# Nyström attention and MLP on one core: another order table, a bf16 landmark softmax, and the first half-sums of k taken the other way round

## The chip, the cores and the metric

The kernel runs on one core of one Trainium2 chip. The core has five engines with a queue each: TensorE (PE, matrix multiply), VectorE (DVE), ScalarE (ACT), GpSimd (POOL) and SyncE (SP, which here only issues transfers). Each engine takes its instructions in the order in which the program lists them; engines wait for one another through semaphores. Transfers between the chip's memory and the core are issued by SP, POOL or ACT and are carried by 16 DMA engines. The metric is the device time of one execution in microseconds (us), the median over runs.

## What is computed

The reference chains a Nyström approximation of attention and a squared-ReLU MLP:

```python
q_lm = q.reshape(B, H, m, S // m, D).mean(axis=3)      # B = H = 8, S = 576, D = 64, m = 32
k_lm = k.reshape(B, H, m, S // m, D).mean(axis=3)
A, Bm, C = sm(q, k_lm), sm(q_lm, k_lm), sm(q_lm, k)    # softmax of a @ b.T / sqrt(D)
Z = Bm.T / (norm_1(Bm) * norm_inf(Bm) + 1e-06)
for _ in range(6):
    Z = 2 * Z - Z @ Bm @ Z
x = (A @ Z @ C @ v)                                    # then (B*S, H*D) = (4608, 512)
out = relu(x @ w_in) ** 2 @ w_out                      # w_in 512 x 2048, w_out 2048 x 512
```

The inputs and the output are float32; the kernel works in bfloat16 with float32 sums and is allowed the difference.

## The kernel before

The 8 batches go through one after the other, and batch b + 1's attention is mixed into batch b's MLP. `attention(b)` does the following, with "turn" counting the repetitions of a tag inside one batch:

- The landmarks. Batches 0 and 1 sum q and k over their segments on PE (`l_sum`, 9 matmuls for each half of the heads, line 544), move the sums out of PSUM (`l_ev`), fold them (`l_fold`, line 554) and duplicate them (`l_dup`). PE also transposes q and k (`tr`, `trk`, line 579, 3 turns of 6 each) and ACT or DVE moves these out (`trev`). Later batches use DVE transposes and adds instead (`hx`, `lmt`, `add9` to `add0h`).
- The 32 x 32 landmark softmax Bm: matmul `bmq`, maximum `nmb`, exponential `Eb` on ACT, reciprocal `rr` of the row sums, product `BB` (line 631), transpose `BTf` (line 633), cast `BTc` (line 634), column sums `cs`, their maximum `mx`, `cc`, reciprocal `rc` (line 651). From these come the first iterate's halves `st0z` (line 667) and `st0p` (line 669, from the matmul `p0`).
- Six Newton steps: matmul `nv` on PE (line 689 in batch 0, 694 later), update `upd` on DVE (line 704), the last one `upd5`.
- Beside them the scores of C (`c_mm`, `nmc`, `c_exp`, transposes `c_tr`, copies `c_ev`), the product with v (`cv`, `cv_ev`) and with Z (`wt`), and the scores of A (`a_mm`, `a_t`, `a_max`, `a_sub`, `a_exp`, `a_sum`, `a_rec`, `a_mul`, transpose `a_xp` into AT).
- Four `g_mm` matmuls multiply the attention's right-hand factor with the four quarters of w_in; eight `g_ev` copies move the result to the tile G.

`mlp_in(b)` then makes 16 blocks: `in_mm` (4 matmuls AT with G, line 948), `relu` (ACT line 965 or DVE line 967) and `square` (ACT line 973, DVE or POOL line 975). `mlp_out(b)` multiplies the blocks with w_out (`o_mm`, line 1020), copies the result (`o_ev`, lines 304 and 306) and stores it.

The order of all this isn't left to a scheduler. `ORDER` is a list of numbers, one for each operation: number // 64 is the operation, number // 8 % 8 its engine (0 PE, 1 ACT, 2 DVE, 3 POOL, 4 SP) and number % 8 its first PSUM bank. A negative number is a run of "fills": matmuls of a zero tile that write to a bank nobody reads (line 455); -480 is 60 of them. `PACE` gives an operation one more wait, on the last instruction of another operation. `Plan.emit` goes through the list and writes out each operation in turn:

```python
for code in order:
    if code < 0:
        self.fill((-code) % 8, (-code) // 8)
        continue
    op, e = self.ops[code // 64], ENGINES[code // 8 % 8]
    ...
        if op.idx in pace:
            wait(mine[0], last[pace[op.idx]])
```

Loads: the first half of batch 0's k comes through SP in two pieces into a float32 stage and is cast by ACT (`first_k`, `cast_k`). Every other load of k and q (two halves, 288 KB each as written), of v (four quarters, 144 KB each), of w_in (four quarters, 512 KB each, line 406) and of w_out (four quarters, line 414) is issued by POOL, in the order of the table, and a POOL load waits for the eighth POOL load before it, whose semaphore it takes over.

Of the kernel before, what the change touches and what calls it, by code (L numbers as in the profile page):

```python
# [8 lines left out]
P = 128  # L9
# [11 lines left out]
M = 32  # L21
# [155 lines left out]
]  # L177

PACE = {
# [908 lines left out]
```

## Time and profile before

| | us |
|---|---|
| median of 3 runs | 260.05 (259.89 to 260.05) |
| the profiled execution | 259.81 |
| its span, first to last instruction | 257.7 |
| PE busy / DVE / ACT / POOL | 245.8 / 206.0 / 199.5 / 143.6 |

The span is what the profile shows; 2.1 us of the execution lie around it. Busy time is the time in which at least one instruction of the engine ran; a fill counts as busy. The views used are the page (busy times, slices, the chain that ended last, groups), the table of stretches (busy time of each engine between two moments), the timeline (instructions in order of time, with the idle time before and what ended it in brackets), and the waits of one engine.

### The profile page before, as it was taken

How to read it: one execution, taken by the hardware profiler on the slowest of the kernel's cores; microseconds unless marked ns; L12 is line 12 of the kernel's file. 1: busy time of each engine (PE TensorE's matmuls, PEld its weight loads, DVE VectorE, ACT ScalarE, POOL GpSimd, SP SyncE). 2: the span in 40 equal slices, each digit the busy share in tenths (PEclk: the TensorE clock that was granted, in tenths of full speed). 3: DMA queues.
4: the chain of work that ended last, by engine and by line, in shares of the span. 5: the costliest groups of instructions: out<-in, count | busy, mean ns of one | idle time of the engine just before them, and what ended most of it. 6: DMA issues, size and time to landing. Idle time of an engine off the chain costs nothing.

```text
span 257.7 us, 7805 instructions
## 1 busy us (share of the span) xinstructions
PE 245.8 (95%) x3018; PEld 147.1 (57%) x3057; DVE 206.0 (80%) x496; ACT 199.5 (77%) x412; POOL 143.6 (56%) x216
## 2 busy tenths in 40 slices
PE   8879899999999999999999999999999999999994
PEld 8766655645654665545545565556645555466552
DVE  0489799999998998999989998888989878944221
ACT  3365799998998899888997798788977778667410
POOL 8446875775694457865587657926172554213300
PEclk9999999999999999999999999999999999999999
DMA  6999999459902980197505972493311432023023
GB/s 158 208 200 194 191 210 205 83 82 169 226 6 47 190 177 20 17 204 140 133 17 84 207 147 55 66 190 96 67 23 23 106 79 48 0 53 91 21 82 124
DMA packets 20468, 28.59 MB, mean 111 GB/s; under 512 B 3280, under 2 KB 11728, under 8 KB 20432
## 3 DMA queue, kind: packets, MB, share of 16 engines
q0 software_dynamic: 13296, 18.06, 43.9%
q1 hardware_dynamic: 6992, 9.90, 13.7%
q8 instruction: 24, 0.39, 0.6%
q10 hardware_dynamic: 144, 0.13, 0.2%
q14 instruction: 12, 0.10, 0.1%
HBM read 36.70 MB, written 9.44 MB: 179 GB/s over the span
## 4 chain that ended last, share of the span: by engine, by line
PE 82%; DMA 6%; DVE 5%; issue 2%; ACT 2%; POOL 1%; DVEq 0%; POOLq 0%; ACTq 0%
PE ps L1020 46%; PE ps L948 23%; DMA kraw<-in_k_dram 3%; PE ps L926 3%; DMA qraw<-in_q_dram 2%; PE ps L725 2%; PE ps L803 2%; PE ps L694 1%; PE ps L781 1%; PE ps L579 1%; PE ps L544 1%; PE ps L455 1%; DVE mxA L888 1%; ACT r L965 1%; POOL w_in_bf L406 1%
## 5 line engine op out<-in xcount | busy, mean ns | idle before, releaser
L1020 PE MATMUL ps<-w_out_bf,gs 128*128 128x512 bf16 (+1 forms) x553 | 138.7, 373 | 2.9 <-issue 1.3
L965 ACT ACTIVATE r<-ps 128x576 bf16<-128x576 f32 x108 | 68.3, 652 | 16.2 <-PE ps L948 13.6
L1020 PEld LDWEIGHTS <-gs 128*128 128x128 bf16 x592 | 53.3, 98 | 47.1 <-issue 7.3
L948 PE MATMUL ps<-AT,G 128*128 128x288 bf16 x512 | 77.5, 286 | 0.5 <-ACT Eb L626 0.2
L948 PEld LDWEIGHTS <-G 128*128 128x128 bf16 x512 | 49.2, 98 | 24.7 <-issue 1.1
L973 ACT ACTIVATE gs<-r 128x576 bf16<-128x576 bf16 x84 | 55.9, 685 | 1.0 <-DVE r L967 0.3
L975 POOL TENSOR_TENSOR gs<-r 128x576 bf16<-128x576 bf16 x24 | 27.6, 1157 | 24.4 <-ACT o L304 9.8
L379 POOL DMA_DIRECT2D vraw<-in_v_dram x32 | 18.2, 571 | 16.8 <-PE ps L725 3.8
L304 ACT CAST G<-ps 128x512 bf16<-128x512 f32 x44 | 23.5, 597 | 3.6 <-PE ps L926 3.5
L304 ACT COPY o<-ps 128x512 f32<-128x512 f32 (+1 forms) x27 | 15.1, 571 | 12.0 <-PE ps L1020 12.0
L967 DVE TENSOR_SCALAR r<-ps 128x576 bf16<-128x576 f32 x20 | 15.0, 751 | 9.8 <-PE ps L948 9.3
L901 POOL TENSOR_TENSOR EA<-EA,rA 128x576 bf16<-128x576 bf16 x15 | 17.4, 1161 | 3.0 <-DVE rA L899 1.1
L533 DVE STREAM_TRANSPOSE qT<-qraw 128x1152 bf16<-128x1152 bf16 x12 | 16.3, 1359 | 0.0
L533 DVE STREAM_TRANSPOSE kT<-kraw 128x1152 bf16<-128x1152 bf16 x12 | 16.2, 1347 | 0.0
L306 DVE CAST G<-ps 128x512 bf16<-128x512 f32 x20 | 13.2, 684 | 2.8 <-PE ps L926 2.8
L306 DVE COPY o<-ps 128x512 f32<-128x512 f32 x10 | 6.8, 685 | 10.6 <-PE ps L1020 10.6
L455 PE MATMUL ps<-zero 128*128 128x128 bf16 x149 | 13.1, 245 | 2.0 <-DVE zero L464 1.1
L890 POOL TENSOR_TENSOR SA<-SA,mxA 128x576 f32<-128x576 f32 x11 | 12.8, 1162 | 3.7 <-DVE Pd L638 2.2
L746 ACT ACTIVATE EC<-ps,nmc 128x288 bf16<-128x288 f32 x24 | 11.7, 499 | 3.8 <-DVE nmc L739 1.5
L704 DVE SCALAR_TENSOR_TENSOR st<-st,ps 128x128 bf16<-128x128 bf16 x40 | 11.0, 276 | 4.1 <-PE ps L694 3.4
L455 PEld LDWEIGHTS <-zero 128*128 128x128 bf16 x149 | 10.8, 112 | 3.6 <-issue 2.2
L884 DVE STREAM_TRANSPOSE SA<-ps 128x576 f32<-128x576 f32 x16 | 11.9, 764 | 1.1 <-PE ps L725 0.6
(146 smaller groups left out, 360.5 us busy)
## 6 DMA issues: line engine op xcount, KB each, us to landing
out_dram<-o SPq DMA_DIRECT2D x126, 64.0 KB, 2.5
qraw<-in_q_dram POOLq DMA_DIRECT2D x16, 288.0 KB, 6.6
vraw<-in_v_dram POOLq DMA_DIRECT2D x32, 144.0 KB, 6.3
kraw<-in_k_dram POOLq DMA_DIRECT2D x15, 288.0 KB, 6.2
w_in_bf<-in_moe_w_in_dram POOLq DMA_DIRECT2D x4, 512.0 KB, 8.1
w_out_bf<-in_moe_w_out_dram POOLq DMA_DIRECT2D x4, 512.0 KB, 9.7
out_dram<-o SPq DMA_DIRECT2D x3, 256.0 KB, 2.3
gs<-in_k_dram SPq DMA_DIRECT2D x2, 288.0 KB, 4.2
```

The source lines that it names most:

```text
L304: nc.scalar.copy(dst, src)
L306: ENG[e].tensor_copy(dst, src)
L379: nc.gpsimd.dma_start(vraws[z][p0:p0 + 32, :, :, :].rearrange("p g t d -> p g (t d)"), src[b].rearrange(order, i=2, t=SEG)[i, :, :, c * NJ ...
L455: mm(ps[:, bank, 0:P], lhsT=zero[:], rhs=zero[:], start=True, stop=True)
L533: add("hx", "DVE", lambda e, nm=nm, raw=raw, i=i: nc.vector.transpose(heads(nm)[:, i, :, :, :].rearrange("p t h r -> p (t h r)"), raw[:, i ...
L901: keep("a_mul", add("a_mul", "POOL DVE", lambda e, part=part, spread=spread: ENG[e].tensor_tensor(part(EA), part(EA), spread(part(rA)), AL ...
L948: mm(t[:, j, 0:HALF], lhsT=G[:, i, f * P:(f + 1) * P], rhs=AT[:, i, j * HALF:(j + 1) * HALF], start=(i == 0), stop=(i == 1))
L965: nc.scalar.activation(r.rearrange("p (j t) -> p j t", j=2), src, AF.Relu)
L967: nc.vector.tensor_scalar(out=r.rearrange("p (j t) -> p j t", j=2), in0=src, scalar1=0.0, scalar2=None, op0=ALU.max)
L973: nc.scalar.activation(dst, r[:], AF.Square)
L975: ENG[e].tensor_tensor(dst, r[:], r[:], ALU.mult)
L1020: mm(one(ok)[:, 0:hi - lo], lhsT=gs[:, f, x0:x0 + P], rhs=w_out_bf[:, f, lo:hi], start=(f == f0), stop=(f == f1 - 1))
```

## The change

Four things change in the code; line numbers after it are one or two lower.

```diff
-    BB = sb.tile([P, 2, M], F32, name="BB")
+    BB = sb.tile([P, 2, M], BF16, name="BB")
...
-    BTf = sb.tile([P, 2, M], F32, name="BTf")
...
-                for i in range(2):
+                for n, i in enumerate((1, 0) if nm == "k" and b == 0 else (0, 1)):
...
-                        writes=[lp, (nm, "lp", i)], acq=None if i else ("n", lp))
+                        writes=[lp, (nm, "lp", i)], acq=None if n else ("n", lp))
...
-            BTf.rearrange("p a m -> p (a m)"), BB.rearrange("p a m -> p (a m)")), reads=["BB"], writes=["BTf"])
-        add("BTc", "DVE ACT", lambda e: copy(e, BTc[:], BTf[:]), reads=["BTf"], writes=["BTc"])
+            BTc.rearrange("p a m -> p (a m)"), BB.rearrange("p a m -> p (a m)")), reads=["BB"], writes=["BTc"])
...
-        add("cs", "DVE", lambda e: nc.vector.reduce_sum(sm["cs"][:], BTf[:], axis=AX.X),
-            reads=["BTf"], writes=["cs"])
+        add("cs", "DVE", lambda e: nc.vector.reduce_sum(sm["cs"][:], BTc[:], axis=AX.X),
+            reads=["BTc"], writes=["cs"])
...
+        add("rq", "DVE", lambda e: nc.vector.tensor_tensor(sm["rq"][:], sm["rr"][:], sm["rc"][:], ALU.mult),
+            reads=["rr", "rc"], writes=["rq"])
...
-        add("st0z", "DVE", lambda e: nc.vector.tensor_tensor(s0[:, :, 1, :], BB[:], bcast(sm["rc"]), ALU.mult),
-            reads=["BB", "rc"], writes=[("st", 0, 1)])
+        add("st0z", "DVE", lambda e: nc.vector.tensor_tensor(s0[:, :, 1, :], Eb[:], bcast(sm["rq"]), ALU.mult),
+            reads=[("Eb", 0), ("Eb", 1), "rq"], writes=[("st", 0, 1)])
```

The fourth is the whole of `ORDER` and `PACE`. The old table has 196 pace waits, the new one 192. Decoded, the beginning of POOL's list reads (kX.h is half h of batch X's k, vX.n a quarter of v, wi and wo the quarters of w_in and w_out, `<-` a pace wait):

```
before: k0.1  q0.0  q0.1  ident  v0.3  q1.0  q1.1  v0.2  v0.0  wi.0  const4  k1.0  v0.1  wi.1<-cc
        a_sub.0  wi.2<-upd.0  k1.1<-a_t.1  a_sub.1  wi.3<-a_sum.0  a_mul.0  wo.0  wo.1  v1.2  k2.1  square ...
after:  q0.0  k0.1  ident  q0.1  const4  q1.0  q1.1  k1.1  k1.0  v0.1  v0.0  v0.2  v0.3<-BB  wi.0<-st0z
        a_sub.0  wi.1<-nmc.0  wi.2<-a_t.1  a_sub.1  wi.3<-upd.3  a_mul.0  a_mul.1  wo.0<-a_xp.0  wo.1  v1.0 ...
```

and the beginning of PE's, up to the first `in_mm`, batch and turn behind the tag, fills in brackets:

```
before: [60] tr.0.0 trk.0.2 l_sum.0.2 l_sum.0.0 l_sum.0.1 tr.0.2 l_sum.0.3 l_fold.0.0 tr.0.1 trk.0.0 trk.0.1
        bmq.0 a_mm.0.0 a_mm.0.1 l_fold.0.1 l_sum.1.2 [6] l_sum.1.3 c_mm.0.0 c_mm.0.1 tr.1.0 p0 [11] nv.0 [8]
        nv.1 [3] c_tr5 nv.2 [4] c_tr4 nv.3 l_sum.1.0 nv.4 [2] cv nv.5 [9] wt.1 wt.0 tr.1.2 [2] g_mm.0 g_mm.1
        [12] g_mm.2 trk.1.0 in_mm.0
after:  [48] tr.0.0 l_sum.0.2 [7] l_sum.0.0 [7] l_sum.0.1 trk.0.0 l_sum.0.3 l_fold.0.0 tr.0.1 trk.0.2 l_fold.0.1
        bmq.0 [2] a_mm.0.0 tr.0.2 trk.0.1 [4] tr.1.2 l_sum.1.2 l_sum.1.3 p0 c_mm.0.1 c_mm.0.0 l_fold.1.1 nv.0
        a_mm.0.1 [4] nv.1 [8] nv.2 [1] c_tr4 [1] c_tr5 nv.3 l_sum.1.0 nv.4 cv nv.5 trk.1.1 l_sum.1.1 wt.0 wt.1
        trk.1.2 tr.1.1 l_fold.1.0 g_mm.0 [5] g_mm.1 bmq.1 trk.1.0 [3] in_mm.0
```

(After the change `l_sum.0.0` is the half of k that POOL loads and `l_sum.0.1` the half from the stage; before, it is the other way round.) In the whole program the fills go from 149 to 109, and the operations that may run on several engines are divided anew, by count:

| operation | ACT | DVE | POOL |
|---|---|---|---|
| square | 84 to 94 | 20 to 18 | 24 to 16 |
| relu | 108 to 104 | 20 to 24 | |
| g_ev | 44 to 46 | 20 to 18 | |
| trev | 5 to 6 | 7 to 6 | |
| o_ev (512 wide) | 25 to 27 | 10 to 8 | |
| c_ev4, c_ev5 | 8 to 6, 4 to 5 | 0 to 2, 4 to 3 | |
| BTc cast / new rq | 7 to 0 / - | 1 to 0 / 0 to 8 | |
| mask | | 39 to 33 | 17 to 23 |
| l_ev, wt_ev, wt_ev0 | 3, 0, 1 to 4, 1, 2 | 1, 1, 1 to 0, 0, 0 | |
| a_sub, a_mul | | 5, 1 to 6, 0 | 11, 15 to 10, 16 |

The small adds of the landmarks move between DVE and POOL in both directions, and the order in which the pieces of output are stored changes with the order of the matmuls before them.

More of the change, by code (lines that the diff above doesn't have):

```diff
@@ L327 @@
     Eb = sb.tile([P, 2, M], F32, name="Eb")
-    BB = sb.tile([P, 2, M], F32, name="BB")
+    BB = sb.tile([P, 2, M], BF16, name="BB")
     sm = {nm: sb.tile([P, 2], F32, name=nm)
-          for nm in ("nmb", "rs", "rr", "cs", "mx", "cc", "rc", "nmc", "rsc", "rcv")}
+          for nm in ("nmb", "rs", "rr", "cs", "mx", "cc", "rc", "rq", "nmc", "rsc", "rcv")}
     rsc = sb.tile([P, 2, 2], F32, name="rscs")
     BTc = sb.tile([P, 2, M], BF16, name="BTc")
-    BTf = sb.tile([P, 2, M], F32, name="BTf")
     BTd = sb.tile([P, 2, NG, M], BF16, name="BTd")
```

311 rows, old and new, of tables (ORDER, PACE) are left out of this document.

## The prediction

> **What bounds the kernel now.** I read the page first, then the table of stretches, then the timeline of the first 28 us. The page's first lines and its chain of the work that ended last:
>
> ```profile
> span 257.7 us, 7805 instructions
> PE 245.8 (95%) x3018; PEld 147.1 (57%) x3057; DVE 206.0 (80%) x496; ACT 199.5 (77%) x412; POOL 143.6 (56%) x216
> ...
> PE 82%; DMA 6%; DVE 5%; issue 2%; ACT 2%; POOL 1%; DVEq 0%; POOLq 0%; ACTq 0%
> ```
>
> PE is busy for 95% and is 82% of the chain. But PE's busy time holds 149 fills, so the table of stretches (us, then busy time and instruction count of PE, PE's weight loads, DVE, ACT, POOL, then clock, DMA share, GB/s) has to say where PE is really the limit:
>
> ```profile
> 0.00:28.00 28.00, 23.09 (x464) 19.37 (x465) 17.38 (x48) 14.27 (x33) 16.98 (x32) 1.00 1.06 190
> 28.00:34.00 6.00, 5.94 (x83) 4.55 (x81) 4.16 (x9) 5.00 (x13) 5.21 (x7) 1.00 1.21 193
> 34.00:40.00 6.00, 5.88 (x47) 3.50 (x46) 5.73 (x17) 5.92 (x13) 3.82 (x6) 1.00 1.13 210
> 40.00:50.00 10.00, 9.95 (x188) 5.75 (x187) 9.80 (x33) 9.94 (x24) 6.03 (x11) 1.00 0.94 158
> 50.00:60.00 10.00, 9.74 (x111) 5.13 (x111) 9.72 (x22) 9.29 (x24) 8.01 (x16) 1.00 0.58 84
> 60.00:80.00 20.00, 19.58 (x256) 11.72 (x259) 19.52 (x47) 19.39 (x37) 13.76 (x20) 1.00 0.57 113
> 80.00:240.00 160.00, 157.24 (x1804) 89.00 (x1832) 137.11 (x322) 133.09 (x270) 87.69 (x128) 1.00 0.48 93
> ```
>
> Three stages with three limits. Up to 28 us no engine is full: the DMA share is at its ceiling (1.06) and the work hangs on landings and on a chain through DVE. From 34 to 80 us PE, DVE and ACT are all full: of 46 us DVE stands idle 1.2 and ACT 1.5. From 80 us PE alone is full: 157.24 of 160, so at most 2.8 us are to be had there. Between them lies 28 to 34, where PE looks full but ACT is idle for 1.00 and DVE for 1.84 us. The first stage in the timeline (start, duration, engine, line, what; in brackets the idle time before and its end):
>
> ```profile
> 1.06 5.59 PE L455 MATMUL ps<-zero 128*128 128x128 bf16 x60 [1.06 <-DVE zero L464]
> ...
> 1.34 0.74 POOL L374 DMA_DIRECT2D kraw<-in_k_dram  x1 [0.82 <-POOLq L1072]
> 2.07 1.10 POOL L374 DMA_DIRECT2D qraw<-in_q_dram  x2
> ...
> 6.75 0.77 POOL L406 DMA_DIRECT2D w_in_bf<-in_moe_w_in_dram  x1 [0.28 <-DMA kraw<-in_k_dram]
> ...
> 7.92 0.51 PE L579 MATMUL ps<-perm,qraw 128*128 128x128 bf16 x6 [1.27 <-DMA qraw<-in_q_dram]
> ...
> 9.71 0.55 POOL L379 DMA_DIRECT2D vraw<-in_v_dram  x1 [0.69 <-DMA qraw<-in_q_dram]
> ...
> 12.15 0.23 PE L604 MATMUL ps<-kdup,qls 128*32 128x32 bf16 x8
> ...
> 14.10 0.24 DVE L633 STREAM_TRANSPOSE BTf<-BB 128x64 f32<-128x64 f32 x1
> 14.27 0.68 PE L544 MATMUL ps<-perm,qraw 128*128 128x128 bf16 x9 [0.43 <-DMA qraw<-in_q_dram]
> ...
> 14.52 0.74 DVE L888 TENSOR_REDUCE mxA<-SA 128x18 f32<-128x576 f32 x1
> ...
> 15.33 0.24 ACT L304 CAST BTc<-BTf 128x64 bf16<-128x64 f32 x1
> ...
> 15.53 0.76 DVE L765 TENSOR_REDUCE nmc<-ps 128x1 f32<-128x576 f32 x1
> ...
> 16.21 0.15 DVE L651 RECIPROCAL rc<-cc 128x2 f32<-128x2 f32 x1
> 16.40 0.23 DVE L667 TENSOR_TENSOR st<-BB,rc 128x64 bf16<-128x64 f32 x1
> ...
> 16.81 0.77 PE L455 MATMUL ps<-zero 128*128 128x128 bf16 x11 [0.88 <-DVE st L669]
> ...
> 17.51 0.24 PE L689 MATMUL ps<-st 32*32 32x64 bf16 x8
> ...
> 22.78 0.21 DVE L714 SCALAR_TENSOR_TENSOR zt<-st,ps 128x64 bf16<-128x64 bf16 x1
> ...
> 24.43 1.08 ACT L304 CAST G<-ps 128x512 bf16<-128x512 f32 x2
> ...
> 25.99 1.16 PE L948 MATMUL ps<-AT,G 128*128 128x288 bf16 x8
> ...
> 27.83 0.68 PE L544 MATMUL ps<-perm,kraw 128*128 128x128 bf16 x9 [0.69 <-DMA kraw<-in_k_dram]
> ```
>
> The reader sees four landings that hold work up (at 7.92, 9.71, 14.27 and 27.83), and the chain bmq (12.15), softmax, first Newton matmul (17.51), last update (22.78), G, first block of the MLP (25.99).
>
> **The change, part by part.** *First loads.* POOL's first transfer in the old table is k0.1, issued at 1.34; it had landed by 6.75, where the ninth load stopped waiting for its semaphore. The new table puts q0.0 in that place, so PE's first transpose can start at about 6.75 instead of 7.92. The second and third transfers of both tables are known too: 7.9 (the old q0.0) and 9.7 (the old q0.1, for which v0.1 waited). In the new table they carry k0.1 and again q0.1. k's sums are then done before q's second half lands, which still sets the pace: l_sum.0.3 at 9.75 and not at about 10.4 (it was queued behind tr.0.2). I take bmq at 11.2 (before 12.15), between 10.9, if every copy is ready, and 11.8, if the trev copies that now share ACT with l_ev come first.
>
> *The softmax chain.* Between BTf and the first Newton matmul DVE did a_max (0.74) and nmc (0.76) within the chain. The new list keeps a_max and puts nmc behind st0p and st0z: 0.76 less. It adds rq, one operation on 2 columns, for which the nearest row is rc with 0.15. The cast BTc (0.24, at 15.33 on ACT) was not last: rc came at 16.21 and so its removal is worth nothing here; p0 has a shorter way, that is all. The bf16 transpose of a bf16 tile has no row of its own; between 0.1 and 0.3 by the f32 one's 0.24, on a path of four steps, it changes nothing I could see. The 11 fills in front of nv.0 (16.81 to 17.51) are gone, 0.70. With DVE's a_t now between nmb and rr (about 0.2 more) the first Newton matmul comes at about 16.1 instead of 17.51: 1.4 earlier.
>
> *And back again.* Behind nv.0 the new list has nmc, nmc, a_t, a_max and a_sum between the updates, one for each step, so a step takes about 1.0 (0.76 and one update of 0.2 to 0.3). cv stands in front of the last Newton matmul and waits for both c_ev copies, which are now both on ACT, behind four exponentials. I get zt at about 22.3 (before 22.78). Then ACT has l_ev.1.0, both wt_ev0, trev.1.1, l_dup.1.0 and only then the first two g_ev, all one after the other, where before ACT and DVE shared the G copies from 24.43 on. By 0.2 + 0.2 + 0.8 + 0.4 + two at 0.54 (half of the 24.43 row) the first `in_mm` is at about 26.0, which is where it was. So the clock gain of the chain is nil at 26 us, bounded by 0.7 earlier and 0.5 later. What remains is work done ahead: l_sum.1.1, two more trk turns, both l_fold.1 and bmq.1 are through, less g_mm.2; some 1.3 us of PE time, and batch 1's landmark softmax can begin 7 us earlier than it did.
>
> *k of batch 1.* k1.1 was POOL's fourteenth load; its landing at 27.83 stopped PE, and behind it waited the chain kT, l_ev, l_dup, bmq.1. The new table has it sixth, in front of v and w_in. At the ceiling of some 200 GB/s (the rows above have 190 to 210) the six POOL loads of 288 KB are 1.7 MB, which takes until about 14 us, and with the tail that q1.1 shows (14.27 in the old order, also as the sixth) at most 15. That stall and its followers are gone. The sizes and the median time to landing:
>
> ```profile
> kraw<-in_k_dram POOLq DMA_DIRECT2D x15, 288.0 KB, 6.2
> w_in_bf<-in_moe_w_in_dram POOLq DMA_DIRECT2D x4, 512.0 KB, 8.1
> ```
>
> In return w_in comes late: wi.0 now waits for st0z, is issued at about 16 instead of 6.75, and a_sub.0, wi.1 and all else on POOL stand behind it. About 4.2 MB have to land by the end of wi.2; at 0.2 MB a us from 4 us on that is 25 us at the earliest, and the old k1.1, with as many bytes up to its end, landed at 27.83. By my count g_mm.2 wants wi.2 at about 26.7. I take it as just hidden, in the middle; uncovered it costs up to 1.1 (27.83 less 26.7).
>
> *Elementwise work.* These rows price the moves (page and groups by shape: count, busy us, mean ns, idle before):
>
> ```profile
> L965 ACT ACTIVATE r<-ps 128x576 bf16<-128x576 f32 x108 | 68.3, 652 | 16.2 <-PE ps L948 13.6
> ...
> L973 ACT ACTIVATE gs<-r 128x576 bf16<-128x576 bf16 x84 | 55.9, 685 | 1.0 <-DVE r L967 0.3
> ...
> L304 ACT CAST G<-ps 128x512 bf16<-128x512 f32 x44 | 23.5, 597 | 3.6 <-PE ps L926 3.5
> ...
> L967 DVE TENSOR_SCALAR r<-ps 128x576 bf16<-128x576 f32 x20 | 15.0, 751 | 9.8 <-PE ps L948 9.3
> ...
> L304 ACT CAST BTc<-BTf 128x64 bf16<-128x64 f32 x7 | 1.7, 242 | 1.1 <-DVE BTf L633 1.1
> L975 DVE TENSOR_TENSOR gs<-r 128x576 bf16<-128x576 bf16 x20 | 9.1, 462 | 1.0 <-ACT r L965 0.9
> ...
> L306 DVE CAST G<-ps 128x512 bf16<-128x512 f32 x20 | 13.2, 684 | 2.8 <-PE ps L926 2.8
> L638 DVE TENSOR_TENSOR Pd<-st,ones_d 128x256 bf16<-128x256 bf16 x31 | 9.4, 304 | 0.6
> ```
>
> ACT: ten squares more (6.85), four relus fewer (2.61), two g_ev more (1.19), seven casts fewer (1.69): +3.7; five further copies net, at 0.6 each, make up to +6.7. DVE: eight rq (1.2), four relus more (3.0), two squares fewer (0.9), two g_ev and two o_ev fewer (2.7), six masks fewer (1.8): about -1.2. Together some +4 over the program, three eighths of it, 1.5, before 80 us, on two engines: 0.75 us each if none is hidden. Before 28 us ACT has 13.7 us idle, which takes most; I charge 0.2, with bounds of 0 and 0.75.
>
> *The fills.* 40 fewer, at 0.07 each (0.77 for 11): 2.8 us of PE time, 12 of them in front of the first landing. They stood in waits, so by themselves they are worth nothing; they become a gain only where PE has something else to do.
>
> The Trainium skill speaks against thinning them: "TensorE: Matmul & The Clock Gate", Part 1, says that the array starts at half rate, needs about 3.4 us of sustained activity and falls back after an idle window of that length. The first row agrees with a slow start (60 fills in 5.59 us, 93 ns each, against 70 ns in the run of 11). By that rule nothing falls back, for the longest idle time above is 1.27 us.
>
> *The sum.* Startup 0; the idle time of 28 to 34 us, the mean of ACT's 1.00 and DVE's 1.84, 1.42 gained, because both were idle for want of batch 1's k; 0.2 charged; nothing behind 80 us, where the positions of the attention operations between the MLP's matmuls are nearly the old ones. 259.81 - 1.4 + 0.2 = 258.6 for a profiled execution; the median of the runs was 0.24 above it, so **258.8**.
>
> **The rivals.** *PE is the limit after all.* If the three engines' fullness in 34 to 80 us is only waiting on one another, PE's lead counts: 1.3 us of work ahead, 0.7 more from the chain, and the 28 fills fewer behind the first landing, 2.0, half of which would be real time: 3.0, so 257.0. For it speaks that the PE list has far fewer fills in the Newton chain; against it that ACT and DVE show 97% there.
>
> *ACT becomes the bound.* Its place is 34 to 80 us, where ACT has 1.5 us free. Three eighths of +6.7 are 2.5; if ACT's idle time there is fixed by waits, only the 1.00 of 28 to 34 can absorb them, and 1.5 come on top: 261.5. It decides as soon as more than 1.2 us of added ACT work are uncovered. Eight squares that POOL no longer makes speak for it; the share of them that lies in the relaxed last batches against it.
>
> *w_in lands late.* The 1.1 us above is paid and cancels most of the gain: 259.9. For it speaks the late issue, against it that nothing but w_in is then under way. *The order does nothing*: what is gained at 28 us waits at 52 or 80 us, where all three engines were full: 260.0.
>
> *A cold array.* Should the warm-up miss the shorter run of 48 fills, some 60 matmuls would go at 93 instead of 70 ns: 1.4 more, 260.2.
>
> **How the numbers follow.** Forecast (257.8 to 259.5) 0.45; PE the limit 0.17; ACT the bound 0.20; w_in late or nothing 0.15; cold array 0.03. About 0.5 us, 0.2%, is what a measurement of this kernel can tell from no change: faster means under 259.5, slower over 260.6. Faster: 0.45 + 0.17 and a little of the others, 0.64. Same: 0.12, from w_in, nothing and the cold array. Slower: ACT's 0.20 and tails, 0.24. The range reaches to the PE case and most of ACT's: 256.6 to 261.2; for the forecast alone it is 257.8 to 259.5.
>
> **What would show it.** First transpose at 6.5 to 7.0; bmq 10.9 to 11.8; first Newton matmul 15.7 to 16.6; first `in_mm` 25.3 to 26.5; no wait of PE for kraw near 28; ACT and DVE over 5.5 of 6 us in 28 to 34. I am wrong on w_in if PE waits for it between 26 and 31, wrong on ACT if its idle time in 34 to 80 is under 0.7 us and PE's is over 2.5, and wrong on the whole if PE's busy share behind 80 us changes by more than 1 us.

## The result, and the profile after

| | before | after |
|---|---|---|
| median, us | 260.06 (20 runs, 259.44 to 261.69) | 258.20 (20 runs, 257.11 to 262.74) |
| the profiled execution, and its span | 259.81, 257.7 | 260.21, 258.5 |

The ratio is 0.9923, with a 95% interval of 0.9901 to 0.9945: 0.8% faster, 1.9 us, where 1.3 us had been forecast. One of the 20 runs of the changed kernel (262.74, at a mean granted clock of 0.978) is in the slow state and is left out of the ratio. The profiled execution is one of the slowest of the changed kernel, 2.0 above its median, and much of what follows is about why.

Not all of the 1.9 us lie in the instructions. Around the span, from the first to the last instruction, there are 2.1 to 2.2 us in each of the 75 runs of the kernel before that were made beside the experiments, and 1.7 to 1.8 us in each of the 20 runs of the changed kernel. That is 0.45 us, for which the forecast had no term, and what it is no view shows. About 1.5 us are gained in the span. The page of the changed kernel:

```profile
span 258.5 us, 7700 instructions
PE 245.5 (95%) x2979; PEld 145.8 (56%) x3017; DVE 202.7 (78%) x495; ACT 202.9 (78%) x418; POOL 137.4 (53%) x211
...
PEclk9999799999999999999999999999999999999999
...
PE 78%; DMA 8%; DVE 5%; ACT 3%; issue 3%; POOL 1%; DVEq 0%; ACTq 0%; POOLq 0%
```

PE's share of the chain fell from 82 to 78%, that of transfers rose from 6 to 8%, and in the fifth slice, near 28 us, the granted clock is low. ACT has 3.4 us more to do, DVE 3.3 less. PE's total is too low, for this trace lacks some matmul records: in the second profile of the same kernel, below, PE has 248.9. The table of stretches, with the columns as before:

```profile
0.00:28.00 28.00, 23.00 (x451) 19.40 (x452) 14.54 (x43) 16.72 (x41) 17.30 (x31) 0.97 1.01 181
28.00:34.00 6.00, 6.00 (x51) 4.06 (x49) 4.77 (x16) 4.89 (x9) 1.65 (x3) 0.87 1.24 208
34.00:40.00 6.00, 5.67 (x85) 3.19 (x85) 5.92 (x17) 5.76 (x11) 3.68 (x7) 1.00 1.17 208
...
80.00:240.00 160.00, 157.15 (x1810) 89.30 (x1836) 137.66 (x331) 133.39 (x271) 82.48 (x122) 1.00 0.46 92
```

In this execution the idle time of 28 to 34 us isn't filled: DVE has 4.77 and ACT 4.89 of 6 (before 4.16 and 5.00), and PE, busy throughout, made 51 matmuls there instead of 83 (the new order makes 68 there in a profile at full clock, shown below). The timeline says what happened ahead of that:

```profile
6.05 0.51 PE L577 MATMUL ps<-perm,qraw 128*128 128x128 bf16 x6
...
11.01 0.23 PE L602 MATMUL ps<-kdup,qls 128*32 128x32 bf16 x8
...
12.89 0.24 DVE L631 STREAM_TRANSPOSE BTc<-BB 128x64 bf16<-128x64 bf16 x1
...
15.56 0.24 PE L688 MATMUL ps<-st 32*32 32x64 bf16 x8
...
15.76 0.77 POOL L404 DMA_DIRECT2D w_in_bf<-in_moe_w_in_dram  x1 [2.06 <-DVE st L666]
...
20.99 0.21 DVE L713 SCALAR_TENSOR_TENSOR zt<-st,ps 128x64 bf16<-128x64 bf16 x1
...
23.53 0.41 PE L928 MATMUL ps<-w_in_bf,WT 64*32 64x512 bf16 x8 [0.75 <-DMA w_in_bf<-in_moe_w_in_dram]
...
26.07 0.62 PE L928 MATMUL ps<-w_in_bf,WT 64*32 64x512 bf16 x8 [1.75 <-DMA w_in_bf<-in_moe_w_in_dram]
...
27.61 2.10 PE L947 MATMUL ps<-AT,G 128*128 128x288 bf16 x8
```

Up to zt (20.99, before 22.78) everything is earlier, by 1.1 to 2.0 us. Then PE waits twice for w_in, 0.75 and 1.75 us, and the first block of the MLP starts at 27.61 instead of 25.99, its eight matmuls in 2.10 us instead of 1.16. The bytes say why w_in is late; GB/s from 10 to 28 us in 40 slices of 0.45 us:

```profile
GB/s 220 205 236 205 200 210 200 225 200 187 202 205 202 205 205 182 52 42 143 193 196 184 182 148 43 80 105 166 205 198 203 198 212 237 191 203 205 196 212 205
```

The flow breaks twice, to about 50 near 17.5 us and near 21 us. Ahead of that POOL, which issues the transfers, had stood still until 15.76, waiting for st0z, and then it made a_sub between two issues.

Whether anything changes behind 80 us is best seen by two marks in PE's list, the first block of batch 2 and the last group of matmuls. In the kernel before:

```profile
79.29 0.65 PE L948 MATMUL ps<-AT,G 128*128 128x288 bf16 x4
...
253.40 1.04 PE L1020 MATMUL ps<-w_out_bf,gs 128*128 128x256 bf16 x8
```

In the changed kernel, this profile:

```profile
80.28 0.65 PE L947 MATMUL ps<-AT,G 128*128 128x288 bf16 x4
...
254.23 1.04 PE L1019 MATMUL ps<-w_out_bf,gs 128*128 128x256 bf16 x8
```

From the one mark to the other it is 174.11 before and 173.95 after. In the other profiles, too, it takes 178.4 us from the first mark to the end of the span in the old order and 178.2 in the new one, whatever happened ahead of it (178.7 and 178.9 in the two runs that change the landmark softmax). So at most 0.2 us are gained behind 80 us, and each profile can be judged by its first mark.

### The profile page after: what moved, and what is told of

Same layout as the page of the kernel before. It is cut to its first block, busy times and chain, and to the rows that moved or that the text cites. A ratio compares the mean times of both kernels' runs of the same rounds, so it can differ in the third digit from the quotient of the medians.

```text
span 258.5 us, 7700 instructions
## 1 busy us (share of the span) xinstructions
PE 245.5 (95%) x2979; PEld 145.8 (56%) x3017; DVE 202.7 (78%) x495; ACT 202.9 (78%) x418; POOL 137.4 (53%) x211
## 4 chain that ended last, share of the span: by engine, by line
PE 78%; DMA 8%; DVE 5%; ACT 3%; issue 3%; POOL 1%; DVEq 0%; ACTq 0%; POOLq 0%
PE ps L1019 43%; PE ps L947 22%; DMA w_in_bf<-in_moe_w_in_dram 3%; DMA w_out_bf<-in_moe_w_out_dram 3%; PE ps L925 3%; PE ps L724 3%; DMA kraw<-in_k_dram 2%; PE ps L802 2%; PE ps L780 1%; PE ps L693 1%; PE ps L542 1%; PE ps L577 1%; POOL SA L889 1%; ACT r L964 1%; ACT EC L745 1%
## 5 line engine op out<-in xcount | busy, mean ns | idle before, releaser
L964 ACT ACTIVATE r<-ps 128x576 bf16<-128x576 f32 x104 | 65.0, 649 | 12.2 <-PE ps L947 9.8
L972 ACT ACTIVATE gs<-r 128x576 bf16<-128x576 bf16 x94 | 61.9, 684 | 2.6 <-DVE r L966 1.9
L974 POOL TENSOR_TENSOR gs<-r 128x576 bf16<-128x576 bf16 x16 | 18.3, 1146 | 27.0 <-DVE r L966 15.1
L303 ACT CAST G<-ps 128x512 bf16<-128x512 f32 x46 | 24.9, 597 | 6.8 <-PE ps L925 4.0
L303 ACT COPY o<-ps 128x512 f32<-128x512 f32 (+1 forms) x29 | 16.4, 574 | 13.1 <-PE ps L1019 11.2
L966 DVE TENSOR_SCALAR r<-ps 128x576 bf16<-128x576 f32 x24 | 17.9, 751 | 7.1 <-PE ps L947 5.0
L635 POOL TENSOR_TENSOR Pd<-st,ones_d 128x256 bf16<-128x256 bf16 x17 | 11.5, 677 | 11.9 <-DVE st L703 5.3
L889 POOL TENSOR_TENSOR SA<-SA,mxA 128x576 f32<-128x576 f32 x10 | 11.6, 1164 | 6.4 <-DVE qs L510 2.9
L453 PE MATMUL ps<-zero 128*128 128x128 bf16 x109 | 11.5, 259 | 1.4 <-DVE zero L462 1.1
L372 POOL DMA_DIRECT2D qraw<-in_q_dram x16 | 9.3, 583 | 5.6 <-DVE kT L305 2.8
```

The costliest lines, as they stand in the source:

```text
L303: nc.scalar.copy(dst, src)
L889: keep("a_sub", add("a_sub", "DVE POOL", lambda e, part=part, spread=spread: ENG[e].tensor_tensor(part(SA), part(SA), spread(part(mxA)), A ...
L964: nc.scalar.activation(r.rearrange("p (j t) -> p j t", j=2), src, AF.Relu)
L966: nc.vector.tensor_scalar(out=r.rearrange("p (j t) -> p j t", j=2), in0=src, scalar1=0.0, scalar2=None, op0=ALU.max)
L972: nc.scalar.activation(dst, r[:], AF.Square)
L974: ENG[e].tensor_tensor(dst, r[:], r[:], ALU.mult)
```

## The experiments

Theories at the start: F is the forecast's (batch 1's k lands early, and the idle time of ACT and DVE at 28 to 34 us is filled), S says that the gain is the earlier first stage, partly given back to late quarters of w_in. Medians in us, ratios against the kernel before on the same chip.

**The changed kernel again**, unedited.

> The changed kernel as it is, for a second profile and as the yardstick of the other three. Both theories expect 257 to 259 us. Theory S (the gain is made in the first 22 us and partly given back to late w_in quarters): a typical profile shows the last Newton update near 21.0 (before 22.78), PE waiting 2 to 3 us for w_in between 23 and 31 us, and the stretch behind 80 us no shorter than before. Theory F (the forecast's: the gain is ACT's and DVE's idle time of 28 to 34 us, which k1.1's landing caused): ACT and DVE together idle under 1.5 us in 28 to 34, before 2.84; no gain left over from the first 26 us.

258.39 (257.02 to 258.88), ratio 0.9919 (0.9889 to 0.9949). The result repeats. In its profile PE waited 0.26 and 1.75 us for w_in, the first block of the MLP started at 27.02, and the clock fell again.

**w_in not held back.** Its five pace waits are taken out (last quarter of v, four quarters of w_in).

```diff
 PACE = {
-    16: 52, 17: 60, 18: 75, 19: 104, 20: 69, 97: 79,
+    97: 79,
```

> The changed kernel without the pace waits of v0.3 and of the four w_in loads, so that POOL issues wi.0 as soon as its semaphore is free (about 11 us) and wi.1 and wi.2 right behind a_sub.0. Theory S: the waits of PE for w_in (2.5 us in the first profile) shrink to under 1.2 and the time falls by 0.8 to 2 us. Theory F, for which w_in is just hidden and its waits in the profile an accident of a slower run: within 0.4 us of the changed kernel. A third way: the pace waits were there to keep POOL's issues from DVE's operations; then the softmax chain gets longer and the time rises by 0.3 to 1 us.

257.39, ratio 0.9886 (0.9857 to 0.9915), 1.0 under the changed kernel beside it. PE's longest waits between 7 and 34 us (in total, times, longest):

```profile
PE ps L802 <- issue: 1.0, 1, 1.0
PE ps L542 <- DMA kraw<-in_k_dram: 0.7, 1, 0.7
```

and the stretch in question:

```profile
28.00:34.00 6.00, 5.73 (x67) 3.82 (x65) 5.90 (x20) 5.76 (x12) 2.34 (x4) 1.00 1.18 190
```

This agrees with theory S. No wait for w_in is left. Instead cv, in two pieces here, waited 1.0 in its middle, with its last 16 matmuls on v to come. DVE and ACT now have 5.90 and 5.76 of 6: once w_in is in time, the idle time that F spoke of is filled.

**The landmark softmax undone**, in the new order: BB in float32, transposed to BTf and cast to BTc by DVE.

```diff
-    BB = sb.tile([P, 2, M], BF16, name="BB")
+    BB = sb.tile([P, 2, M], F32, name="BB")
+    BTf = sb.tile([P, 2, M], F32, name="BTf")
...
+            nc.vector.transpose(BTf.rearrange("p a m -> p (a m)"), BB.rearrange("p a m -> p (a m)"))
+            nc.vector.tensor_copy(BTc[:], BTf[:])
```

> The changed kernel with the landmark softmax written and transposed in float32 again and the cast back (one more DVE copy of about 0.2 us for each batch, directly behind the transpose). Theories S and F: 0 to 0.3 us more, since in batch 0 the copy stands in the chain to the first Newton matmul (0.2) and later batches have slack. A rival for which the bf16 softmax is what pays: 1 us or more is lost.

259.53, ratio 0.9969 (0.9946 to 0.9993): 1.1 over the changed kernel, and the intervals just overlap. That is more than theories S and F allowed, but the cast in batch 0's chain isn't the reason. The first Newton matmul is at 16.12 against 15.59 in the profile beside it, but bmq, ahead of the edit, is already at 11.58 against 10.90, because PE had waited 0.79 us for k; from bmq to the Newton matmul it takes 4.5 us here and 4.7 there. Seven of the 12 runs had a mean granted clock of 0.992 or 0.993, against one of six beside it. Behind the first mark this profile takes 178.9 us where the others of the new order take 178.2. What the 1.1 us are made of is open.

**The same part alone, in the old order:** BTc's operation emits nothing, and st0z's makes rq first.

```diff
+            nc.vector.tensor_tensor(sm["rq"][:], sm["rr"][:], sm["rc"][:], ALU.mult)
+            nc.vector.tensor_tensor(s0[:, :, 1, :], Eb[:], bcast(sm["rq"]), ALU.mult)
...
-        add("BTc", "DVE ACT", lambda e: copy(e, BTc[:], BTf[:]), reads=["BTf"], writes=["BTc"])
+        add("BTc", "DVE ACT", lambda e: None, reads=["BTf"], writes=["BTc"])
```

> The kernel before with the landmark softmax of the changed kernel in its old order: BB bf16, transposed straight into BTc, no cast, st0z from Eb and rq, both on DVE in the place of the old st0z. Forecast: worth nothing by itself (rc was last, the cast ran beside it, rq costs 0.15): ratio 0.999 to 1.001. Theory S2 (by the run that undid this part, which was about 1.1 slower than the changed kernel): the shorter chain and the eight casts less are worth 0.5 to 1.1, ratio 0.996 to 0.998. Cost case: rq between rc and st0z delays the first Newton matmul by 0.15 and the time rises by as much, ratio 1.0006.

260.10, ratio 1.0015 (0.9991 to 1.0039). By itself the part is worth nothing, as the forecast had it; what it saves in the new order was measured only with a cast on DVE, where the old kernel had seven of the eight casts on ACT.

**The halves of k in the old order.**

```diff
-                for n, i in enumerate((1, 0) if nm == "k" and b == 0 else (0, 1)):
+                for n, i in enumerate((0, 1)):
...
 ORDER = [
-    592, 32, 344, 280, 72, 472, 720, -384, 2628, 2696, 2309, -56, 1606, 160, 200, 784,
+    592, 32, 344, 280, 72, 472, 720, -384, 2628, 2696, 2309, -56, 160, 200, 1606, 784,
```

> The changed kernel with the stage half of k summed first, as before, and k0.1 second, at the same two places of PE's list. The second cast ends near 8.0 us and k0.1 had landed by 7.8. Theories S and F: first half-sum 0.2 us later, nothing by the time of bmq, so within 0.3 us of the changed kernel. The rival (landing order matters): bmq 0.3 us or more later and the time up by as much.

257.87, ratio 0.9926 (0.9890 to 0.9961): no different from the changed kernel. Its profile caught an execution at full clock, the fastest of the ten and 1.1 under their median, and so shows what this order does at its best:

```profile
28.00:34.00 6.00, 5.83 (x68) 4.01 (x67) 5.87 (x20) 5.88 (x11) 2.33 (x4) 1.00 1.24 206
...
80.00:240.00 160.00, 159.91 (x1810) 89.59 (x1809) 135.83 (x321) 133.17 (x268) 83.21 (x122) 1.00 0.46 92
```

Its first mark:

```profile
76.85 0.65 PE L947 MATMUL ps<-AT,G 128*128 128x288 bf16 x4
```

ACT and DVE are filled, and the mark is 2.4 us ahead of the kernel before, though w_in still cost PE 1.8.

**More fills in the wait for w_in**, 24 of them.

```diff
-    -42, 7362,
+    -234, 7362,
```

> The changed kernel with 24 more fills (about 1.7 us at 0.07 each) behind the 5 between the first and the second g_mm, where PE waited 1.75 us for the second quarter of w_in. Theory C (cold array): the two waits of PE for w_in (0.75 and 1.75 us) let the granted clock fall in the stretch of 28 to 34 us (0.87 and 0.90 in the two profiles of the changed kernel, 1.00 in the two variants), and that is what parts its runs; with PE kept busy the clock is 1.00 in 28 to 34, no run shows 0.993 as its mean, and the median falls from 258.3 to 257.5-257.9. Theory D (the drop is not tied to this wait): the profile or some of the runs still show 0.993, the median stays within 258.1 to 258.6. If the fills outlast the wait, the second g_mm comes later than at 25.6 and the median rises by up to 0.4.

258.37, ratio 0.9925 (0.9909 to 0.9940). The clock was 1.00 from 28 to 34 in the profile and at least 0.998 in five of the six runs, but the sixth had 0.993 and took 261.72, which theory C had ruled out, and the five have a median of 258.24: the time did not fall to C's 257.5 to 257.9. The place agrees with theory C, the rest with D; six runs are too few to tell a cure from luck.

**The kernel before, with the second half of batch 1's k early.**

```diff
-    592, 32, 72, 280, 344, 160, 408, 472, 784, 720, -480, 2628, 2181, 2256, 2704, 2310, 1048, 1496, 1560, 200,
+    592, 32, 72, 280, 344, 160, 408, 472, 784, 720, -480, 2628, 2181, 2256, 2704, 2310, 1048, 1496, 1560, 1432, 200,
...
-    18: 57, 19: 63, 20: 99, 22: 104, 97: 60,
+    18: 57, 19: 63, 20: 99, 97: 60,
```

> The kernel before with one load moved: the second half of batch 1's k is issued right behind q of batch 1, without its pace, instead of behind the third quarter of w_in. Theory F (the forecast's main term: the late k is what keeps ACT and DVE idle between 28 and 34 us): PE's wait for kraw near 28 is gone, ACT and DVE are over 5.5 of 6 us in 28 to 34, and the median is about 1.4 below the kernel before, ratio 0.9946. Theory S (the gain of the change is made by the whole first stage being earlier): the wait of 0.69 goes, but no more than that follows, ratio 0.997 to 1.000. A third way: v of batch 0, now behind this load, comes late for cv, and the time is up to 0.5 above the kernel before.

259.83, ratio 0.9989 (0.9977 to 1.0001). PE's list around 28 us:

```profile
26.34 0.41 PE L929 MATMUL ps<-w_in_bf,WT 64*32 64x512 bf16 x8 [1.02 <-DMA w_in_bf<-in_moe_w_in_dram]
...
28.00 0.67 PE L544 MATMUL ps<-perm,kraw 128*128 128x128 bf16 x9
```

and the stretches:

```profile
28.00:34.00 6.00, 5.93 (x83) 4.57 (x81) 4.11 (x10) 5.77 (x14) 5.15 (x7) 1.00 1.19 192
...
80.00:240.00 160.00, 159.84 (x1833) 88.92 (x1832) 137.14 (x323) 133.03 (x270) 87.40 (x128) 1.00 0.47 93
```

The wait for k at 28 us is gone, and a wait for w_in of 1.02 stands in its place: the bytes moved forward pushed w_in back. ACT's idle time there went (5.77 of 6, before 5.00), but DVE is as idle as it was (4.11 and 4.16). In the old list batch 1's landmark work stands where it stood: its matmul bmq is at 32.95 here and at 32.79 in the kernel before. Theory F's cause, the landing alone, falls.

**w_in spread:** the halves of k in the old order, v's last quarter unpaced, the first quarter of w_in behind BB, the second ahead of a_sub (its number is taken out further down), the others unpaced.

```diff
-    16: 52, 17: 60, 18: 75, 19: 104, 20: 69, 97: 79,
+    17: 52, 97: 79,
...
-    5128, 4816, 5192, 1112, -37, 4100, 4176, -69, 4228, 4936, -13, 5381, 6232,
+    5128, 4816, 5192, 1112, -37, 4100, 4176, -69, 4228, 4936, -13, 5381, 1176, 6232,
```

> The changed kernel with the halves of k in the old order, and w_in issued so that v lands first and the queue never runs dry: the last quarter of v without its pace, the first quarter of w_in behind BB instead of st0z, the second in front of a_sub, the third and fourth without pace. Theory S (from about 21 us on only w_in's landing holds PE): no wait of PE for w_in, cv still near 19.8, the first in_mm at 24.6 to 25.2 against 26.0 and 25.8 of the two variants that had one of the edits, and the median 256.6 to 257.2. Rival (the bytes are the limit, at 0.2 MB a us the order of the transfers only moves the wait): PE waits for w_in, v or kraw by 1 us or more in sum between 18 and 30, median 257.4 to 258.0. F (the startup's clock does not matter for the end): 258.2 to 258.5, as the changed kernel.

257.41, ratio 0.9902 (0.9880 to 0.9924), the same as with w_in simply early, and what its rival had: cv waits 0.74 for v. **v ahead of w_in** is that kernel with the first quarter of w_in behind rc.

```diff
-    17: 52, 97: 79,
+    17: 57, 97: 79,
```

> The variant with w_in spread, with its first quarter waiting for rc instead of BB, about 1.2 us later, so that v of batch 0 shares the queue with less of w_in. Theory S (any wait between 18 and 26 us moves the end): cv's wait of 0.74 for v goes, the first in_mm is at 25.0 or earlier, the median 256.6 to 257.1. Rival (the bytes are the limit: 3.68 MB landed in the 18 us from 10 to 28, 204 GB/s, the ceiling): the wait moves from v to w_in at the second or third g_mm, and the median stays within 257.2 to 257.8.

256.69 (255.70 to 257.30), ratio 0.9863 (0.9832 to 0.9893), better than both kernels. The timeline of PE; the last line is the first mark:

```profile
19.36 0.75 PE L802 MATMUL ps<-vraw,ECT 64*32 64x64 bf16 x72 [0.24 <-ACT ECT L303]
...
23.59 0.41 PE L928 MATMUL ps<-w_in_bf,WT 64*32 64x512 bf16 x8 [0.62 <-DMA w_in_bf<-in_moe_w_in_dram]
...
76.25 0.65 PE L947 MATMUL ps<-AT,G 128*128 128x288 bf16 x4
```

and its flow from 10 to 28 us:

```profile
GB/s 220 195 220 226 210 195 210 215 200 200 197 210 197 205 205 227 165 199 200 209 209 198 205 209 205 209 207 200 207 209 230 196 200 200 205 212 205 207 203 205
```

The flow never breaks now, cv runs in one piece, and w_in costs 0.9 instead of 2.5. The rival's "the bytes only move the wait" is half right (a wait went back to w_in), but it got smaller, and theory S has the median. (By the medians this is 1.5 to 1.7 under the changed kernel, with three edits at once; the halves of k, alone, made no difference.)

**Fewer fills in the kernel before:** the 32 behind the first in_mm are left out; the negative numbers of those six runs go from the table.

> The kernel before without the 32 fills that stand behind the first in_mm (runs of 2, 3, 4, 8, 8 and 7, between 31 and 60 us; the first 117 stay). Theory P (PE is the limit from 28 us on, and fewer fills are a main part of the gain): at 0.07 each 2.2 us of PE time, of which at least half comes back, ratio 0.992 to 0.996. Theory W (they stand where PE would wait anyway): ratio 0.999 to 1.001, and PE's idle time between 28 and 60 us goes up by about 2 us. A third way: without them the clock falls in some runs and the time rises by 0.5 or more.

259.72, ratio 1.0001 (0.9978 to 1.0024). The fills' time turns into idle time:

```profile
40.00:50.00 10.00, 8.73 (x172) 4.86 (x171) 9.80 (x32) 9.97 (x24) 6.20 (x10) 1.00 0.93 157
50.00:60.00 10.00, 9.59 (x101) 4.74 (x101) 9.72 (x23) 9.31 (x25) 7.77 (x15) 1.00 0.67 100
```

PE is idle 1.27 and 0.41 here (before 0.05 and 0.26), DVE and ACT are as full as they were. PE's fullness from 31 to 60 us was not the limit of the kernel before.

**Batch 1's landmark softmax held back**, on the variant with w_in spread; 18 operations are moved (and v1.2's pace, which hung on one of them).

```diff
-    -42, 7362, 8968, 9680, 8712, 9860, 9936, 8773, 7960,
+    -42, 7362, 8968, 9680, 8712, 8773, 7960,
...
-    8216, -13, 15938, 15504, 16132, 15624, 10256, 15816, 16008, 10384, 16320, 16514, 10448, 16710, 16200, 13252,
+    15816, 16008, 16320, 16514, 16710, 16200, 9860, 9936, 9992, 10056, 15696, 10128, 10192, 10256, 16072, 15888,
```

> The variant with w_in spread (257.41), with batch 1's landmark softmax, from bmq to the first half-iterates and their masks, held back behind the relu of in_mm 5, some 6 us later and just in time for the first Newton matmul of batch 1; all of PE's other work stays where it was. Theory F (the forecast's main term: the idle time of ACT and DVE in 28 to 34 us, filled by batch 1's landmark work, is what the change gains): in 28 to 34 DVE or ACT is idle for over 1 us again, and the median is 258.4 to 258.9. Theory P (what counts is PE's own work done ahead and its fewer waits): idle time comes back in 28 to 34 but the median stays within 257.1 to 257.8. A third way: the later chain stops PE at the first Newton matmul of batch 1, near 38 us, by more than 1 us, and the median is over 258.9.

262.04, ratio 1.0062 (1.0033 to 1.0091), 4.6 over its base, worse than either theory had it:

```profile
31.83 0.23 DVE L617 TENSOR_REDUCE nmb<-ps 128x2 f32<-128x64 f32 x1 [2.19 <-PE ps L605]
...
34.47 0.75 DVE L966 TENSOR_SCALAR r<-ps 128x576 bf16<-128x576 f32 x1
...
35.27 0.37 PE L453 MATMUL ps<-zero 128*128 128x128 bf16 x2 [3.57 <-DVE r L966]
```

DVE stood 2.19 us for bmq, and a relu behind the landmark operations on DVE's queue, wanted by PE's next fill, came at 34.47; PE stood for 3.57. The edit put the chain in front of that relu, so the run shows what a late chain does to a queue that keeps order, but doesn't tell F from P.

**More work for ACT**, on the best variant: two of its squares made twice.

```diff
+                    if b == 0 and f in (0, 4):
+                        nc.scalar.activation(dst, r[:], AF.Square)
                     nc.scalar.activation(dst, r[:], AF.Square)
```

> The variant with v landing before w_in (256.69), with two of ACT's squares of batch 0 (blocks 0 and 4, near 25.9 and 29.4 us) made twice: 1.37 us more of ACT's work, nothing else changed. Theory F (from 28 us on the engines that do the elementwise work are the limit, so that filling their idle time is the gain; also the forecast's rival that ACT is the bound): ACT's idle time from 28 to 50 us is 0.10, 0.02 and 0.44, so 0.8 to 1.4 of it comes through, median 257.5 to 258.1. Theory P (PE's own work is the limit): no more than 0.2 comes through, median 256.5 to 256.9.

257.21, ratio 0.9886 (0.9858 to 0.9915), 0.5 over its base of 0.9863, with intervals that overlap. Of 1.37 us at most some 0.5 came through, between the two theories; and of the 0.67 us between the first marks of the two profiles (76.92 and 76.25) 0.22 were there at the first block of the MLP (24.70 and 24.48), ahead of the doubled squares. Nothing clear of the noise is shown.

## Why the prediction was nearly right

The time forecast was 258.8, the time measured 258.2. By its own steps:

- *First loads and chain.* Right in direction, too small. First transpose 6.05 (forecast 6.75, range 6.5 to 7.0: the moment at which a later load stopped waiting only bounds the landing from above); bmq 11.01 (11.2); first Newton matmul 15.56 (16.1); zt 20.99 (22.3). From Newton matmul to zt it takes 5.4 us, hardly more than before (5.3); the forecast's 1.0 for each of the six steps was too much, a step takes 0.9.
- *Startup 0 at the first in_mm, near 26.0.* The figure fits the variant with the old halves (25.85), but by two errors that cancel: the chain was quicker and w_in later. In the two profiles of the changed kernel it is 27.61 and 27.02.
- *w_in just hidden.* **This step failed.** It asked only for the third quarter and took the flow to be at its ceiling from 4 us on. PE waited for the first and second, 2.5 us in all, ahead of the stretch (26 to 31) in which the forecast said to look, because the flow broke off while POOL waited. Not holding w_in back gave 1.0 us, and a better order 1.5 to 1.7. The rival "w_in lands late" had the cost about right (1.1), but not the total of 259.9: the gain that it was to cancel was larger than the forecast's.
- *k of batch 1.* The stall is gone. But the reason given for the 1.42 us, that ACT and DVE were idle "for want of batch 1's k", is not what the runs show: with k early and the old list only 0.3 (by the ratio) to 0.5 us (by the medians) came, and DVE's idle time stayed. What fills it is the list, in which batch 1's landmark work comes 6 to 8 us earlier, as its matmul bmq shows (kernel before, changed kernel, variant with the old halves):

```profile
32.79 0.22 PE L607 MATMUL ps<-kdup,qdup 64*32 64x32 bf16 x8
...
26.42 0.33 PE L605 MATMUL ps<-kdup,qdup 64*32 64x32 bf16 x8
...
25.17 0.23 PE L605 MATMUL ps<-kdup,qdup 64*32 64x32 bf16 x8
```

Where w_in and the clock cost less, in the variant with the old halves, DVE went from 4.16 to 5.87 of 6 and ACT from 5.00 to 5.88, a mean of 1.3, close to the term.
- *The elementwise work.* ACT rose by 3.4 and DVE fell by 3.3 (forecast +3.7 to +6.7 and -1.2). ACT's rival didn't occur: ACT is idle for 2.2 of the 46 us from 34 to 80, where the rival needed under 0.7. Its price of one for one isn't borne out either: of 1.37 us added where ACT was fullest at most some 0.5 came through.
- *The fills.* "By themselves worth nothing" held. The rival in which PE's fewer fills are real time falls for 31 to 60 us.
- *Nothing behind 80 us* held, to 0.2 us between the marks. The bound of 2.8 us given for that stretch was a misreading: 157.24 of 160 busy in the first trace is 159.84 in the trace of e6, where nearly the same list runs, and the changed kernel's 157.15 is 159.90 in its second profile; what looked like idle time was records that the traces lack.
- *A cold array*, at 0.03, came true in some of the runs, for a reason that the forecast didn't have: in the two profiles that show it, not the shorter warm-up but the waits for w_in stand ahead of it.

The sum was right within 0.6 us, but luck has a part in that. With w_in hidden or nearly so, as the forecast took it to be, the time is 1.4 to 2.1 us lower than forecast: 257.39, 257.41 and 256.69 are the medians of the three kernels that issue w_in earlier, in whose profiles no more than 0.9 us of waiting for it was left. A gain that was larger than forecast and a cost that was left out came out near the forecast; and 0.45 us of the gain lie outside the span.

Where the larger gain is made, two instants of each profile show. From the first block of the MLP to the first mark it takes 53.30 us in the kernel before, and 52.42 and 52.59 in its variants with k early and with fewer fills. In the variants of the new order whose clock held it takes 51.0 to 51.8 (51.00 with the old halves; 52.2 with the work added for ACT), and in the two profiles of the changed kernel 52.67 and 51.94, with the slow clock in it. So the new order gains between these two instants, and the first block of the changed kernel comes 1.0 to 1.6 us later than before, not earlier. The filled idle time of ACT and DVE is some 1.3 of the 2.3 us by which the variant is shorter there. Work was also done ahead: before 28 us the variant's ACT is busy for 17.82 instead of 14.27 us, its DVE for 16.00 instead of 17.38. How the rest divides between the two is open, and that the filled idle time itself makes the gain is argued, not shown: the run made for it didn't separate them.

The clock takes a part of this back, but not only from the changed kernel. In the runs with a mean granted clock of 0.998 or more the median of the changed kernel is 257.85 and that of the kernel before 260.0, a difference of 2.2 instead of 1.9; runs at 0.991 to 0.993 also occur in the kernel before, 10 of the 75.

## What to carry to other kernels

A transfer moved forward takes its bytes from the next ones: count what every consumer behind it needs, quarter by quarter, and look at GB/s for gaps that the issuing engine's own waits make. A full engine isn't yet the limit: take its filler away, or double one of its operations, and see whether the end moves. And when a kernel's profiled run lies well above its median, read the clock row before explaining its stretches.

## What the hardware showed that had not been expected

In two profiles the clock of the array fell after waits shorter than had been thought to matter. The changed kernel in finer stretches (PE's busy time is the second group, the clock the third figure from the end):

```profile
22.00:24.00 2.00, 1.25 (x24) 0.88 (x22) 1.86 (x4) 1.36 (x5) 1.96 (x3) 1.00 1.16 187
24.00:26.00 2.00, 0.33 (x5) 0.24 (x4) 0.72 (x2) 1.07 (x2) 1.51 (x3) 1.00 1.25 210
26.00:28.00 2.00, 1.93 (x27) 1.59 (x27) 0.69 (x2) 1.14 (x5) 0.00 (x0) 0.54 1.25 204
28.00:29.00 1.00, 1.00 (x6) 0.61 (x5) 0.69 (x2) 0.19 (x1) 0.61 (x2) 0.50 1.23 205
29.00:30.00 1.00, 1.00 (x18) 0.67 (x15) 0.18 (x1) 0.97 (x2) 0.47 (x1) 0.72 1.26 210
30.00:31.00 1.00, 1.00 (x15) 0.65 (x15) 0.96 (x4) 0.73 (x2) 0.00 (x0) 1.00 1.22 203
```

After waits of 0.75 and 1.75 us, PE busy for 1.58 of 4 us, the array ran at half its clock for some 3.5 us. In the second profile of the changed kernel it did so after waits of 0.26 and 1.75. But such waits don't always bring it about: in the run with the float32 softmax PE waited 0.25 and 1.75 us at the same place, in the variant with the old halves 1.64, and both kept 1.00. Of the 19 runs of the changed kernel without the one of 262.74, five had a mean granted clock of 0.993 and took 259.52 on average; the other fourteen, at 0.998 or more, had a median of 257.85. The 0.7% of 258 us that the clock lacked are 1.8 us, and the difference is 1.7. Of the 48 runs of the three kernels whose profiles have a wait of 1.6 us or more for w_in (these two and the changed kernel), 16 were at 0.993 or less; of the 75 of the kernel before 10 were, and two of the six with w_in not held back, one of them at only 257.30. So such runs are more frequent where the wait is, but the wait isn't their only occasion, and for runs without a profile the place of the drop isn't known. None of the 12 runs of the two kernels in which v lands ahead of w_in was under 0.999. The run with the late landmarks shows the same after a longer wait, from 31.70 to 35.27:

```profile
34.00:35.00 1.00, 0.00 (x0) 0.00 (x0) 0.97 (x4) 1.00 (x2) 0.36 (x1) 0.67 1.19 212
35.00:36.00 1.00, 0.73 (x17) 0.26 (x17) 0.22 (x1) 0.04 (x1) 1.00 (x3) 0.50 1.15 218
...
40.00:41.00 1.00, 1.00 (x20) 0.72 (x18) 0.56 (x3) 1.00 (x3) 0.03 (x1) 0.50 0.64 84
41.00:42.00 1.00, 1.00 (x18) 0.47 (x7) 0.98 (x4) 1.00 (x3) 0.58 (x2) 0.91 0.85 133
```

The Trainium skill, "TensorE: Matmul & The Clock Gate", Part 1, has the clock at half or full and nothing between, falling back after an idle window of about 3.4 us and coming back after as long a busy one; the prediction took from it that nothing would fall back. The half rate agrees with these rows, and so do the 3.5 us of slow clock in the changed kernel. An idle window in the strict sense doesn't: no wait there lasted over 1.75 us, PE only had little to do for about as long as the window. With the late landmarks the array stayed at half for nearly 7 us, with PE busy for the last 5.9 of them. The same part of the page calls the window free-running, one that doesn't begin with the work; a busy stretch would then have to wait for the next whole window. The lengths agree: in steps of 0.1 us the slow spells last from 26.1 to 29.6, from 25.8 to 29.2 in the second profile, and here from 34.3 to 41.2, that is 3.4, 3.4 and 6.8, once and twice the page's figure. That would also let the same waits lower the clock in one execution and not in another; no run here shows where the windows lie.

The bf16 transpose took 0.24 us (12.89 in the timeline above), as the float32 one had: half the bytes saved no time.
